# A head's 48 output columns as a 64-row tile of 32 and a shared tile of 16, and x in three PSUM banks

## The chip, the cores and the metric

The kernel runs on one core of a Trainium2 chip. The metric is the time of one execution in microseconds (us), the median of several runs. A smaller number is better. TensorE (PE) does matrix products, VectorE (DVE) and ScalarE (ACT) do elementwise work, GpSimd (POOL) and SyncE (SP) issue DMAs here.

## What is computed

A gated linear attention over 768 steps for 4 batches of 8 heads of width 48, then two feed-forward layers over the 3072 tokens. The inputs are float32.

```python
# attention: q, k, v, alpha are (4, 8, 768, 48)
for t in range(S):
    state = alpha[:, :, t, :, None] * state + np.einsum('bhd,bhe->bhde', k[:, :, t], v[:, :, t])
    y[:, :, t] = np.einsum('bhd,bhde->bhe', q[:, :, t], state)
x = y.transpose(0, 2, 1, 3).reshape(3072, 384)
# layer 1 (384 -> 1536 -> 384)
g = x @ w_gate
x = (g * (1.0 / (1.0 + np.exp(-g))) * (x @ w_val)) @ w_out
# layer 2: x / rms(x) * rms_g first, then the same with its own weights
```

## The kernel before

**Attention.** The work is cut into 24 chunks: 6 blocks of 128 steps for each of 4 batches, with all 8 heads in a chunk. Heads go in 4 pairs (`NP`); a pair's first head lies on partitions 0 to 63 and its second on 64 to 127, of which 48 each are used. Inside a chunk the product over steps is split by levels 1, 2, 4, 8, 16, 32, 64 (`LEVELS`): at level b the second half of each run of 2b steps attends to the first half. The first 6 chunks do all seven levels; the other 18 do the five from 4 up and get the terms of short distance from DVE instead (`CDS`).

For a level, `scores` makes a 64 x 64 score block per head on PE, in tiles of 64 rows by 32 columns; DVE masks it or ACT copies it to SBUF (`masks`, `copies_p`), as P. `outputs` then multiplies v (`vlt`) by P into the PSUM tile `y`, which holds the transposed output x: 384 output columns as partitions of three groups of 128, by 128 steps. A pair has 96 output columns, three blocks of 32 (`blocks32`). The middle block mixes both heads, so v lies in SBUF padded with zeros to 96 columns for either head, and every product uses all 128 rows: 12 matrix products per level, three per pair. `own_terms` writes the terms of the chunk's own steps into `y` by a transpose and adds q times the state (12 more products, with the padded state `Sd`). `kp`, `kt` and `kv` make k transposed and k^T v for the state (`state`), which the chunk of the same batch four later uses. `split_x` copies `y` out as a float32r high part (`xhi`, ACT) and a low part (`xlo`, DVE); that is the input of layer 1.

PSUM before: `y` has one bank, the pool `ps2` has two that scores, `kp`, `kv` and two small tiles of the norm take in turn, and the feed-forward layers have the other five (`g`, `v`, `o0` to `o2`).

**Feed-forward.** Layer 1 goes over 7 blocks of 3 or 4 chunks, layer 2 over 6 blocks of 4. Each block goes over 12 slices of the 1536 hidden columns, and for each slice PE does pieces g, v and o; in layer 1, from the second block on, and in layer 2 each piece is nine products in float32r (high and low parts). The first block uses float32 with six instructions on the chip in a piece. The weights of layer 1 are unpacked by ACT and DVE first (`conv`, lines 150 to 172), and this runs beside the first chunks.

**Order.** All engines run in the order in which the code is written. A chunk is a list of steps T = 0 to 23; `slot` runs the step T of one chunk and T - 12 of the next. Chunks 0 to 2 run alone, and later ones have their slots placed between the pieces of the block before (`run`, `mlp_points`). The steps that matter here: scores of levels 1 to 8 at T = 6 (which is T = 18 of the chunk before), masks at 7, 8 and 10, scores of levels 16 to 64 at 9, `kp` at 12, `kt` at 13, `own_terms` and the first outputs at 14, `kv` and the other outputs at 16, the high part of x and the state at 17, the low part at 18. Waits between engines are put in by the framework from the tiles that instructions share.

Of the kernel before, what the change touches and what calls it, by code (L numbers as in the profile page):

```python
# [55 lines left out]
class Kernel:  # L56


    def __init__(self, tc, ctx, qka, vl, vlx, vn, qn, dirx, w1, w2, g2, mask, ident, zero, out):
# [7 lines left out]
        self.ps2 = self.pool("ps2", 2, space=PSUM)  # L67
# [185 lines left out]

    def scores(self, n, ls):

        nc = self.nc
        qk = self.qk[n % 2]
        sc_all = self.ps2.tile([128, 4, NP, 32], F32, tag="sc", name="sa" if ls[0] < 4 else "sb")
        out = {}
        for i, l in enumerate(ls):  # L260
            b = LEVELS[l]
            if b < CDS[n]:
                continue
            if b < 64:
                sc = out[l] = sc_all[:, i]
                kc = self.kc.pop((n, l))
                qc, kc = kc[:, 0], kc[:, 1]
            else:
                sc = out[l] = sc_all[:, 2:4].rearrange("s g p t -> s (g p t)").rearrange("s (p t) -> s p t", p=NP)
# [33 lines left out]
    def blocks32(self):  # L303

        for cb in range(3 * NP):
            yield cb // 3, slice(32 * (cb % 3), 32 * (cb % 3) + 32), cb // 4, 32 * (cb % 4)

    def own_terms(self, n):

        nc = self.nc  # L310
        Y = self.Y = self.ps.tile([128, KT, C], F32, tag="y", name="y")
        yn = self.yn.pop(n)
        for k in range(KT):
            nc.tensor.matmul(out=Y[:, k], lhsT=yn[:, 128 * k:128 * k + 128], rhs=self.ident, is_transpose=True,  # L314
                             start=(k == 0), stop=False, skip_group_check=True)
        if n >= B:
            for p, e, kt, o in self.blocks32():
                nc.tensor.matmul(out=Y[o:o + 32, kt], lhsT=self.Sd[:, p].rearrange("d h e -> d (h e)")[:, e],  # L318
                                 rhs=self.qk[n % 2][:, 0, p], start=False, stop=False, skip_group_check=True)

    def outputs(self, n, ls):
        for l in ls:
            b = LEVELS[l]
            if b < CDS[n]:
                continue
            pt = self.P.pop((n, l))
            for p, e, kt, o in self.blocks32():
                ov = self.Y[o:o + 32, kt].rearrange("e (j u i) -> e j u i", u=2, i=b)[:, :, 1]
                self.nc.tensor.matmul(out=ov, lhsT=self.vlt[l][:, p, e], rhs=pt[:, p],  # L329
                                      start=False, stop=False, skip_group_check=True)  # L330
        if n == CDS.index(4) - 1:
            self.pxfree = True

    def kv(self, n):

        nc = self.nc
        kv = self.ps2.tile([128, NP, D], F32, tag="sc", name="kv")
        kt, vn = self.kt.pop(n), self.vnt.pop(n)
        for p in range(NP):
            for h in range(2):  # L340
                for o in (64 * h, 64 * h + 32):
                    nc.tensor.matmul(out=kv[o:o + 32, p], lhsT=kt[:, p, o:o + 32], rhs=vn[:, p, h],  # L342
                                     start=True, stop=True, skip_group_check=True)
        self.kvt = kv
# [11 lines left out]
    def split_x(self, m, part):  # L356
        Y = self.Y
# [73 lines left out]
    def chunk(self, n, T):  # L431
# [5 lines left out]
        if T == 12 and more:  # L437

            kp = self.kp = self.ps2.tile([128, NP, 128], F32, tag="sc", name="kp")
            for p in range(NP):  # L440
                nc.tensor.transpose(out=kp[:, p], in_=self.qk[n % 2][:, 1, p], identity=self.ident)  # L441
        if T == 14:
            self.own_terms(n)
            self.outputs(n, range(4))
# [38 lines left out]
        if T == 11 and n >= B:  # L483
            for h in range(2):
                o = slice(64 * h, 64 * h + 64)
                nc.scalar.activation(out=self.Sd[o, :, h], in_=self.Sc[n % B][o], func=AF.Copy)
        if T == 13 and more:
            kt = self.kt[n] = self.a1.tile([128, NP, 128], F32, tag="kt", name="kt")
            nc.scalar.activation(out=kt, in_=self.kp, func=AF.Copy)
# [16 lines left out]
    def norm_steps(self, j):  # L506
# [16 lines left out]
        ss = self.ps2.tile([128, MB], F32, tag="sc", name="ss")  # L523
# [17 lines left out]
        rb = self.ps2.tile([128, NW], F32, tag="sc", name="rb")  # L541
# [125 lines left out]
    def run(self):  # L667
# [16 lines left out]
        self.vlt = [v(0, 96), v(384, 96)] + self.vlt  # L684
# [73 lines left out]
def _layout(inputs):  # L758
    q, k, v, a = (np.asarray(inputs[n]) for n in ("q", "k", "v", "alpha"))
    con = np.ascontiguousarray  # L760
# [11 lines left out]
    for b in LEVELS:  # L772
        x = vt.reshape(NCH, C // (2 * b), 2, b, NP, 2, D)[:, :, 0].reshape(NCH, 64, NP, 2, D)
        o = np.zeros_like(x[:, :, :, 0])
        z = [np.stack([x[:, :, :, 0], o], axis=3), np.stack([o, x[:, :, :, 1]], axis=3)]
        vl.append(np.concatenate(z, axis=1).reshape(NCH, 128, NP, 2 * D))
# [8 lines left out]
    for pre in ("moe_", "moe2_"):  # L785
        wg, wv, wo = (np.asarray(inputs[pre + s]) for s in ("w_gate", "w_val", "w_out"))
        w = [x.reshape(KT, 128, NF, 128).transpose(2, 1, 0, 3).reshape(NF, 128, 384) for x in (wg, wv)]
# [21 lines left out]
```

## Time and profile before

| | |
|---|---|
| median of 3 runs | 1138.23 us (1137.38 to 1142.36) |
| the profiled execution | 1136.99 us |
| its span, first to last instruction | 1135.2 us |
| PE busy | 1084.1 us (95%) |
| DVE busy | 656.4 us (58%) |
| ACT busy | 417.7 us (37%) |
| DMA moved | 112.54 MB |

The profile is of one execution. What lies outside its span is 1.8 us. An engine's busy time counts time in which at least one of its instructions is under way; instructions of PE overlap. A float32 product shows as two instructions in the profile, a float32r one as one.

### The profile page before, as it was taken

The page shows a single profiled execution, that of the slowest core. Times are in us where ns is not written, and L with a number is a line of the kernel's source. Part 1 is how long each engine was busy: PE and PEld are TensorE (multiplying, and loading weights), DVE is VectorE, ACT ScalarE, POOL GpSimd, SP SyncE. Part 2 cuts the span into 40 slices and gives each one's busy share as a digit, 9 for nine tenths or more (in the row PEclk, how much of TensorE's full clock was granted, in tenths as well). Part 3 has the DMA queues.
Part 4 walks back from the last instruction along what each step waited for, and adds up shares of the span by engine and source line. Part 5 has one row for each costly group of instructions (what it writes and reads, how often), then busy time and mean ns, then how long its engine had stood idle before and what let it go on. Part 6 is the DMA issues. An engine that isn't in the chain of part 4 may idle for free.

```text
span 1135.2 us, 29428 instructions
## 1 busy us (share of the span) xinstructions
PE 1084.1 (95%) x12864; PEld 901.0 (79%) x12864; DVE 656.4 (58%) x1361; ACT 417.7 (37%) x749; POOL 46.5 (4%) x81
## 2 busy tenths in 40 slices
PE   2679999999999999999999999999999999999997
PEld 2555569999999988887888888888888888888886
DVE  4789876877678777676746887723322323233221
ACT  3465624543344443343324354432231222322212
POOL 2012000000000000000000000000000000000000
PEclk9689999999999999999999999999999999999999
DMA  9677535443454463444315243110000000100000
GB/s 278 207 213 238 159 99 148 114 125 105 127 166 139 125 173 106 116 127 139 105 58 207 99 152 113 42 56 1 28 28 1 29 28 1 56 1 1 29 1 28
DMA packets 56033, 112.54 MB, mean 99 GB/s; under 512 B 7392, under 2 KB 40672, under 8 KB 55904
## 3 DMA queue, kind: packets, MB, share of 16 engines
q1 hardware_dynamic: 50592, 89.02, 27.1%
q0 software_dynamic: 5312, 21.63, 5.5%
q8 instruction: 101, 1.65, 0.6%
q14 instruction: 28, 0.23, 0.1%
HBM read 97.65 MB, written 12.98 MB: 97 GB/s over the span
## 4 chain that ended last, share of the span: by engine, by line
PE 85%; DVE 2%; DMA 2%; ACT 1%; issue 1%; SPq 0%; DVEq 0%; ACTq 0%; POOLq 0%
PE g L605 25%; PE v L605 25%; PE o L646 25%; PE y L329 3%; PE sb L277 2%; PE y L318 1%; PE sa L277 1%; PE kv L342 1%; PE y L314 1%; PE kp L441 1%; PE rb L544 0%; DMA x2d<-ev 0%; DMA ydd<-yd 0%; PE ss L525 0%; ACT ev L566 0%
## 5 line engine op out<-in xcount | busy, mean ns | idle before, releaser
L615 DVE TENSOR_TENSOR s<-s,v 128x512 f32<-128x512 f32 (+1 forms) x156 | 100.8, 646 | 368.4 <-PE v L605 365.1
L605 PE MATMUL g<-xhi,w 128*128 128x512 f32 (+1 forms) x864 | 282.8, 381 | 0.0
L605 PE MATMUL v<-xhi,w 128*128 128x512 f32 (+1 forms) x864 | 281.8, 380 | 0.0
L646 PE MATMUL o<-hh,w 128*128 128x512 f32 (+1 forms) x864 | 208.7, 377 | 0.0
L621 ACT ACTIVATE hh<-s 128x512 fp32r<-128x512 f32 (+1 forms) x144 | 87.2, 606 | 278.6 <-DVE s L615 278.4
L612 ACT ACTIVATE s<-g 128x512 f32<-128x512 f32 (+1 forms) x156 | 88.1, 565 | 259.3 <-PE g L605 250.6
L605 PEld LDWEIGHTS g<-xhi,w 128*128 128x128 f32 x864 | 161.2, 188 | 27.9
L605 PEld LDWEIGHTS v<-xhi,w 128*128 128x128 f32 x864 | 161.3, 188 | 27.1
L646 PEld LDWEIGHTS o<-hh,w 128*128 128x128 f32 x864 | 160.0, 188 | 25.9
L605 PE MATMUL g<-xlo,w 128*128 128x512 f32 (+1 forms) x432 | 162.6, 376 | 0.0
L605 PE MATMUL v<-xlo,w 128*128 128x512 f32 (+1 forms) x432 | 162.6, 376 | 0.0
L646 PE MATMUL o<-hl,w 128*128 128x512 f32 (+1 forms) x432 | 120.6, 386 | 1.2 <-ACT ev L566 0.8
L627 DVE TENSOR_TENSOR hl<-s,hh 128x512 fp32r<-128x512 f32 (+1 forms) x144 | 94.4, 656 | 42.1 <-ACT hh L621 37.7
L605 PEld LDWEIGHTS g<-xlo,w 128*128 128x128 f32 x432 | 81.2, 188 | 12.8
L605 PEld LDWEIGHTS v<-xlo,w 128*128 128x128 f32 x432 | 81.2, 188 | 12.3
L646 PEld LDWEIGHTS o<-hl,w 128*128 128x128 f32 x432 | 77.7, 188 | 16.6 <-ACT ev L566 2.3
L229 DVE TENSOR_TENSOR qk<-qk,bpb 128x512 f32<-128x512 f32 x96 | 65.7, 685 | 7.0 <-ACT kc L252 4.7
L252 ACT ACTIVATE kc<-qk 128x512 f32<-128x512 f32 x72 | 45.4, 631 | 61.0 <-DVE qk L229 60.3
L329 PE MATMUL y<-pt,vl 128*32 128x64 f32 x2880 | 52.1, 225 | 2.2 <-issue 2.2
L329 PEld LDWEIGHTS y<-pt,vl 128*32 128x32 f32 x2880 | 47.1, 115 | 3.8 <-issue 3.8
L298 ACT ACTIVATE pt<-sb 32x128 f32<-32x128 f32 x96 | 25.7, 268 | 41.1 <-DVE pt L288 40.1
L229 DVE TENSOR_TENSOR qk<-qk,bpa 128x512 f32<-128x512 f32 x48 | 33.0, 687 | 5.0 <-ACT px L252 3.3
(104 smaller groups left out, 1037.7 us busy)
## 6 DMA issues: line engine op xcount, KB each, us to landing
vl<-vl SPq DMA_DIRECT2D x120, 192.0 KB, 4.9
qk<-qka SPq DMA_DIRECT2D x48, 288.0 KB, 5.0
room<-w POOLq DMA_DIRECT2D x36, 384.0 KB, 5.2
dir<-dirx SPq DMA_DIRECT2D x54, 192.0 KB, 3.2
wraw<-w SPq DMA_DIRECT2D x18, 384.0 KB, 3.9
room<-w SPq DMA_DIRECT2D x18, 384.0 KB, 3.9
vn<-vn SPq DMA_DIRECT2D x24, 192.0 KB, 4.2
x2in<-x2d SPq DMA_DIRECT2D x6, 768.0 KB, 4.3
```

The source lines that it names most:

```text
L229: self.nc.vector.tensor_tensor(out=v, in0=v, in1=sub(t, o, [(1, 2), (2, nb), (0, b)]), op=ALU.mult)
L252: self.nc.scalar.activation(out=sub(t, 0, [(NP * 64, 2), (b, NP * 64 // b), (1, b)]), in_=v, func=AF.Copy)
L277: nc.tensor.matmul(out=sc[o:o + 32, p], lhsT=kc[d, p, gs], rhs=qc[d, p, gs if b < 64 else slice(0, 64)], start=True, stop=True, skip_group ...
L298: nc.scalar.activation(out=self.pt32[o:o + 32, :, g], in_=out[NL - 2][o:o + 32], func=AF.Copy)
L314: nc.tensor.matmul(out=Y[:, k], lhsT=yn[:, 128 * k:128 * k + 128], rhs=self.ident, is_transpose=True, start=(k == 0), stop=False, skip_gro ...
L329: self.nc.tensor.matmul(out=ov, lhsT=self.vlt[l][:, p, e], rhs=pt[:, p], start=False, stop=False, skip_group_check=True)
L605: nc.tensor.matmul(out=ps[:, :N], lhsT=a, rhs=x, start=(q == 0), stop=(q == len(ops) - 1))
L612: nc.scalar.activation(out=s[:, :N], in_=g[:, :N], func=AF.Silu)
L615: nc.vector.tensor_tensor(out=s[:, :N], in0=s[:, :N], in1=v[:, :N], op=ALU.mult)
L621: nc.scalar.activation(out=hh[:, :N], in_=s[:, :N], func=AF.Copy)
L627: nc.vector.tensor_tensor(out=hl[:, :N], in0=s[:, :N], in1=hh[:, :N], op=ALU.subtract)
L646: nc.tensor.matmul(out=O[gj][i][:, :N], lhsT=a[:, 128 * i:128 * i + 128], rhs=x[:, :N], start=(f == 0 and q == 0), stop=(f == NF - 1 and q ...
```

## The change

The PSUM tile `Y` is made once, with three banks of 512 columns. Columns 0 to 127 of each bank hold x; what used the pool `ps2` lies in the rest of the same banks: scores (`place_sc`), `kp`, `kv` and, later, the norm's two tiles. The pool `ps2` is gone.

A head's 48 output columns are a block of 32 of its own and one of 16. The block of 32 is a product over that head's 64 rows alone; the two blocks of 16 of a pair share one block of 32 columns and one product over 128 rows. The second head's columns are turned by 16 on the host (`_layout`), in v and in the rows of the first layer's weights, so that the order of output columns in x fits. v needs 64 columns a pair in SBUF in place of 96, and `Sd` 32 in place of 96. The count of products stays 12 per level: four of 128 rows, then eight of 64 rows. Each call of `outputs` does all shared ones of its levels first and then all of 64 rows. The terms of the state come the same way, inside `outputs`.

```diff
-        self.ps2 = self.pool("ps2", 2, space=PSUM)
+        self.Y = self.ps.tile([128, 3, NW], F32, name="Y")
+        self.kvt = self.Y[:, 2, C:C + NP * D].rearrange("d (p e) -> d p e", e=D)
+        self.kp = self.Y[:, 0:2, C:3 * C]
...
-        self.vlt = [ac.tile([128, NP, 2 * D], F32, name=f"vl{i}") for i in range(NL - NX)]
+        self.vlt = [ac.tile([128, NP, 64], F32, name=f"vl{i}") for i in range(NL - NX)]
         self.Sc = [ac.tile([128, NP, D], F32, name=f"S{b}") for b in range(B)]
-        self.Sd = ac.tile([128, NP, 2, D], F32, name="Sd")
+        self.Sd = ac.tile([128, NP, 32], F32, name="Sd")
...
+    def place_sc(self, l):
+        i, c = (l // 2, 1 + l % 2) if l < 4 else (l - 4, 3)
+        return i, slice(c * C, c * C + C)
...
-    def blocks32(self):
-
-        for cb in range(3 * NP):
-            yield cb // 3, slice(32 * (cb % 3), 32 * (cb % 3) + 32), cb // 4, 32 * (cb % 4)
-
     def own_terms(self, n):
 
-        nc = self.nc
-        Y = self.Y = self.ps.tile([128, KT, C], F32, tag="y", name="y")
         yn = self.yn.pop(n)
         for k in range(KT):
-            nc.tensor.matmul(out=Y[:, k], lhsT=yn[:, 128 * k:128 * k + 128], rhs=self.ident, is_transpose=True,
-                             start=(k == 0), stop=False, skip_group_check=True)
-        if n >= B:
-            for p, e, kt, o in self.blocks32():
-                nc.tensor.matmul(out=Y[o:o + 32, kt], lhsT=self.Sd[:, p].rearrange("d h e -> d (h e)")[:, e],
-                                 rhs=self.qk[n % 2][:, 0, p], start=False, stop=False, skip_group_check=True)
-
-    def outputs(self, n, ls):
+            self.nc.tensor.matmul(out=self.Y[:, k, 0:C], lhsT=yn[:, C * k:C * k + C], rhs=self.ident, is_transpose=True,
+                                  start=True, stop=False, skip_group_check=True)
+
+    def outputs(self, n, ls, own=False):
+        mm = lambda o, a, x: self.nc.tensor.matmul(out=o, lhsT=a, rhs=x, start=False, stop=False, skip_group_check=True)
+        ls = [l for l in ls if LEVELS[l] >= CDS[n]]
+        pt = {l: self.P.pop((n, l)) for l in ls}
+        q = self.qk[n % 2][:, 0]
+
+        def y(p, part, l=None):
+            j = 3 * p + part
+            t = self.Y[32 * (j % 4):32 * (j % 4) + 32, j // 4, 0:C]
+            return t if l is None else t.rearrange("e (j u i) -> e j u i", u=2, i=LEVELS[l])[:, :, 1]
+        own = own and n >= B
+        if own:
+            for p in range(NP):
+                mm(y(p, 1), self.Sd[:, p], q[:, p])
         for l in ls:
-            b = LEVELS[l]
-            if b < CDS[n]:
-                continue
-            pt = self.P.pop((n, l))
-            for p, e, kt, o in self.blocks32():
-                ov = self.Y[o:o + 32, kt].rearrange("e (j u i) -> e j u i", u=2, i=b)[:, :, 1]
-                self.nc.tensor.matmul(out=ov, lhsT=self.vlt[l][:, p, e], rhs=pt[:, p],
-                                      start=False, stop=False, skip_group_check=True)
-        if n == CDS.index(4) - 1:
+            for p in range(NP):
+                mm(y(p, 1, l), self.vlt[l][:, p, 32:64], pt[l][:, p])
+        halves = [(p, h, slice(64 * h, 64 * h + 64)) for p in range(NP) for h in range(2)]
+        if own:
+            for p, h, d in halves:
+                mm(y(p, 2 * h), self.Sc[n % B][d, p, 16 * h:16 * h + 32], q[d, p])
+        for l in ls:
+            for p, h, d in halves:
+                mm(y(p, 2 * h, l), self.vlt[l][d, p, 0:32], pt[l][d, p])
+        if n == CDS.index(4) - 1 and NL - 1 in ls:
...
-        kv = self.ps2.tile([128, NP, D], F32, tag="sc", name="kv")
+        kv = self.kvt
...
             self.own_terms(n)
-            self.outputs(n, range(4))
+            self.outputs(n, range(4), own=True)
...
-                nc.scalar.activation(out=self.Sd[o, :, h], in_=self.Sc[n % B][o], func=AF.Copy)
+                nc.scalar.activation(out=self.Sd[o, :, 16 * h:16 * h + 16], in_=self.Sc[n % B][o, :, 32 - 32 * h:D - 32 * h], func=AF.Copy)
```

Below, rows of the program's order (line, operation, output <- inputs, output shape, xcount) show three places; a bracket names the engine or DMA queue whose signal the instruction waits for. In the changed file the lines of the same functions are a few higher.

PE at T = 14 of a chunk with five levels, before: the transposes of the own terms, the state's product, then levels 4 and 8.

```order
L314 MATMUL y<-ident,yn 128x128 [waits DMASW7_49]
L314 MATMUL y<-ident,yn 128x128 x2
L318 MATMUL y<-qk_91,Sd 32x128 x12
L329 MATMUL y<-pt,vl_92 32x16x4 [waits DMAHW1_49]
L329 MATMUL y<-pt,vl_92 32x16x4 x11
L329 MATMUL y<-pt,vl_93 32x8x8 [waits DMAHW2_49]
L329 MATMUL y<-pt,vl_93 32x8x8 x11
```

The same place of another such chunk, with the change: the first rows of four are the shared products, the last three rows those of 64 rows.

```order
L312 MATMUL Y<-ident,yn 128x128 [waits DMASW1_49,Activation_49]
L312 MATMUL Y<-ident,yn 128x128 x2
L316 MATMUL Y<-qk_88,Sd 32x128 x4
L316 MATMUL Y<-pt,vl_90 32x16x4 [waits DMAHW2_49]
L316 MATMUL Y<-pt,vl_90 32x16x4 x3
L316 MATMUL Y<-pt,vl_91 32x8x8 [waits DMAHW3_49]
L316 MATMUL Y<-pt,vl_91 32x8x8 x3
L316 MATMUL Y<-qk_88,S_97 32x128 x8
L316 MATMUL Y<-pt,vl_90 32x16x4 x8
L316 MATMUL Y<-pt,vl_91 32x8x8 x8
```

Twelve products a level have become four and eight, the eight of all levels stand together at the end, and the transposes wait for ACT, whose last use of the tile ahead of them is the copy of k transposed (`kt`, T = 13).

PE at the scores of chunk 5 (T = 6), between pieces g, v and o of the first block, before:

```order
L605 MATMUL v<-x_460,x_122 128x384 [waits DVE_49]
L605 MATMUL v<-x_460,x_122 128x384 x2
L277 MATMUL sa<-px 32x32 [waits PE_49]
L277 MATMUL sa<-px 32x32 x31
L277 MATMUL sa<-kc 32x32 x16
L277 MATMUL sa<-kc 32x32 [waits Activation_49]
L277 MATMUL sa<-kc 32x32 x15
L646 MATMUL o_1244<-s,x_122 128x384
```

The same place with the change:

```order
L612 MATMUL v<-x_453,x_120 128x384 [waits DVE_49]
L612 MATMUL v<-x_453,x_120 128x384 x2
L282 MATMUL Y<-px 32x32 [waits DVE_49]
L282 MATMUL Y<-px 32x32 x31
L282 MATMUL Y<-kc 32x32 x16
L282 MATMUL Y<-kc 32x32 [waits Activation_49]
L282 MATMUL Y<-kc 32x32 x15
L653 MATMUL o_1224<-s,x_120 128x384
```

The scores stand where they stood, and the first of them waits for DVE in place of PE itself. The last DVE instruction ahead of them that uses the tile is the low part of x of chunk 4 (`xlo`).

DVE at the state and the low part of x (T = 17 and 18) of a later chunk, before:

```order
L353 TENSOR_TENSOR S_99<-S_99,bpb 128x192
L354 TENSOR_TENSOR S_99<-S_99,kv 128x192 [waits DVE_49,PE_49]
L229 TENSOR_TENSOR qk_91<-qk_91,bpb 128x2x16x16 [waits Activation_49]
L221 TENSOR_TENSOR bpb<-bpb 128x8
L384 TENSOR_TENSOR dir<-dir 128x96
L384 TENSOR_TENSOR pr<-dir 128x96 [waits DVE_49]
L374 TENSOR_TENSOR xlo<-y,xhi 128x3x128 [waits Activation_49]
```

The same place with the change:

```order
L360 TENSOR_TENSOR S_97<-S_97,bpb 128x192
L361 TENSOR_TENSOR S_97<-S_97,Y 128x192 [waits DVE_49,Activation_49]
L231 TENSOR_TENSOR qk_89<-qk_89,bpb 128x2x16x16
L223 TENSOR_TENSOR bpb<-bpb 128x8
L391 TENSOR_TENSOR dir<-dir 128x96
L391 TENSOR_TENSOR pr<-dir 128x96 [waits DVE_49]
L381 TENSOR_TENSOR xlo<-Y,xhi 128x3x128
```

The addition of k^T v to the state waits for ACT (the high part of x, which ACT copies just ahead from the same tile) where it waited for PE's `kv`; the rest of the order is the same. The scores of level 16 (T = 9) get a wait for DVE's mask of level 8 (T = 8) in the same way.

## Rows read from the trace of the kernel before

**Rows 1.** The page: the chain that ended last, by engine.

```profile
PE 85%; DVE 2%; DMA 2%; ACT 1%; issue 1%; SPq 0%; DVEq 0%; ACTq 0%; POOLq 0%
```

**Rows 2.** Stretches: length, busy (xcount) PE, PEld, DVE, ACT, POOL; clock, DMA, GB/s.

```profile
0.00:70.00 70.00, 32.96 (x1370) 29.29 (x1372) 42.41 (x93) 30.42 (x53) 10.53 (x24) 0.80 0.84 250
155.00:600.00 445.00, 443.29 (x7828) 385.93 (x7817) 314.94 (x777) 173.58 (x370) 23.43 (x36) 1.00 0.46 126
```

**Rows 3.** Timeline of PE, chunk 13: start, us from first to last end.

```profile
352.55 0.86 PE L318 MATMUL y<-qk,Sd 128*32 128x128 f32 x24
353.23 0.85 PE L329 MATMUL y<-pt,vl 128*32 128x64 f32 x48
354.01 0.45 PE L605 MATMUL g<-xhi,w 128*128 128x384 f32 x1
...
355.78 0.55 PE L342 MATMUL kv<-vn,kt 128*32 128x48 f32 x32
356.14 1.19 PE L329 MATMUL y<-pt,vl 128*32 128x64 f32 x72
357.26 0.45 PE L605 MATMUL v<-xhi,w 128*128 128x384 f32 x1
```

**Rows 4.** A stretch of 0.035 us there: busy PE of tile y (instructions under way).

```profile
356.13:356.17 0.04, 0.02 (x4) 1.00 0.00 0
```

**Rows 5.** Timeline of chunks 4 and 5: PE with DVE and ACT.

```profile
121.90 0.49 PE L314 MATMUL y<-ident,yn 128*128 128x128 f32 x3
...
124.69 0.58 ACT L489 ACTIVATE kt<-kp 128x512 f32<-128x512 f32 x1
...
134.07 0.72 PE L277 MATMUL sa<-px 64*32 64x32 f32 x62
...
137.65 0.55 DVE L374 TENSOR_TENSOR xlo<-y,xhi 128x384 fp32r<-128x384 f32 x1
```

**Rows 6.** Timelines at the states of chunks 1, 2 and 3: DVE and ACT.

```profile
51.61 0.69 DVE L229 TENSOR_TENSOR qk<-qk,bpb 128x512 f32<-128x512 f32 x1 [0.34 <-ACT kc L252]
...
52.21 0.49 ACT L368 ACTIVATE x<-y 128x384 f32<-128x384 f32 x1 [0.64 <-PE y L329]
...
68.06 0.48 ACT L368 ACTIVATE x<-y 128x384 f32<-128x384 f32 x1
68.20 0.69 DVE L229 TENSOR_TENSOR qk<-qk,bpb 128x512 f32<-128x512 f32 x1 [0.64 <-ACT kc L252]
...
99.30 0.35 DVE L350 COPY S<-kv 128x192 f32<-128x192 f32 x1
...
100.19 0.48 ACT L372 ACTIVATE xhi<-y 128x384 fp32r<-128x384 f32 x1
```

**Rows 7.** Timelines of chunks 1 and 2: DVE's masks of levels 8 and 16.

```profile
42.54 0.42 DVE L288 TENSOR_TENSOR pt<-sb,mask 128x256 f32<-128x256 f32 x1 [2.71 <-PE sb L277]
...
57.09 0.42 DVE L288 TENSOR_TENSOR pt<-sa,mask 128x256 f32<-128x256 f32 x1
...
58.48 0.42 DVE L288 TENSOR_TENSOR pt<-sb,mask 128x256 f32<-128x256 f32 x1
```

**Rows 8.** Stretch of chunk 2's scores of levels 16 to 64: busy PE.

```profile
55.32:57.28 1.96, 1.94 (x96) 0.50 0.27 46
```

**Rows 9.** Timeline of chunk 14 and the scores of chunk 15.

```profile
376.99 0.35 DVE L354 TENSOR_TENSOR S<-S,kv 128x192 f32<-128x192 f32 x1
377.86 0.49 ACT L372 ACTIVATE xhi<-y 128x384 fp32r<-128x384 f32 x1 [0.56 <-PE y L329]
379.69 0.55 DVE L615 TENSOR_TENSOR s<-s,v 128x384 f32<-128x384 f32 x1 [1.21 <-PE v L605]
380.16 0.55 DVE L374 TENSOR_TENSOR xlo<-y,xhi 128x384 fp32r<-128x384 f32 x1
...
381.08 1.07 PE L277 MATMUL sa<-kc 64*32 64x32 f32 x64
```

More of the change, by code (lines that the diff above doesn't have):

```diff
@@ L264, in scores @@
             if b < 64:
-                sc = out[l] = sc_all[:, i]
+                sc = out[l] = self.Y[:, *self.place_sc(l)].rearrange("s (p t) -> s p t", p=NP)
                 kc = self.kc.pop((n, l))
@@ L268, in scores @@
             else:
-                sc = out[l] = sc_all[:, 2:4].rearrange("s g p t -> s (g p t)").rearrange("s (p t) -> s p t", p=NP)
+                sc = out[l] = self.Y[:, 2, C:3 * C].rearrange("s (p t) -> s p t", p=NP)
                 qc, kc = qk[:, 0, :, 64:128], qk[:, 1, :, 0:64]
@@ new lines, in outputs @@
+    def outputs(self, n, ls, own=False):
[11 more added lines that the diff above has]
+                mm(y(p, 1), self.Sd[:, p], q[:, p])
+        for l in ls:
+            for p in range(NP):
[4 more added lines that the diff above has]
+                mm(y(p, 2 * h), self.Sc[n % B][d, p, 16 * h:16 * h + 32], q[d, p])
+        for l in ls:
+            for p, h, d in halves:
+                mm(y(p, 2 * h, l), self.vlt[l][d, p, 0:32], pt[l][d, p])
+        if n == CDS.index(4) - 1 and NL - 1 in ls:
@@ L342, in kv @@
                     nc.tensor.matmul(out=kv[o:o + 32, p], lhsT=kt[:, p, o:o + 32], rhs=vn[:, p, h],
-                                     start=True, stop=True, skip_group_check=True)
-        self.kvt = kv
+                                     start=False, stop=True, skip_group_check=True)
     def state(self, n):
@@ L437, in chunk @@
         if T == 12 and more:
-            kp = self.kp = self.ps2.tile([128, NP, 128], F32, tag="sc", name="kp")
             for p in range(NP):
-                nc.tensor.transpose(out=kp[:, p], in_=self.qk[n % 2][:, 1, p], identity=self.ident)
+                nc.tensor.transpose(out=self.kp[:, p // 2, C * (p % 2):C * (p % 2) + C], in_=self.qk[n % 2][:, 1, p],
+                                    identity=self.ident)
         if T == 14:
             self.own_terms(n)
-            self.outputs(n, range(4))
+            self.outputs(n, range(4), own=True)
         if T == 16:
@@ L522, in norm_steps @@
         yield
-        ss = self.ps2.tile([128, MB], F32, tag="sc", name="ss")
+        ss = self.Y[:, 0, 0:MB]
         for c in range(MB):
@@ L540, in norm_steps @@
         yield
-        rb = self.ps2.tile([128, NW], F32, tag="sc", name="rb")
+        rb = self.Y[:, 1]
         for c in range(MB):
@@ L759, in _layout @@
     q, k, v, a = (np.asarray(inputs[n]) for n in ("q", "k", "v", "alpha"))
+    turn = np.roll(np.arange(D), 16)
+    v = np.stack([v[:, 0::2], v[:, 1::2][..., turn]], axis=2).reshape(v.shape)
+    head = np.arange(DM).reshape(NP, 2, D)
+    order = np.stack([head[:, 0], head[:, 1][:, turn]], axis=1).ravel()
     con = np.ascontiguousarray
@@ L786, in _layout @@
         wg, wv, wo = (np.asarray(inputs[pre + s]) for s in ("w_gate", "w_val", "w_out"))
+        if pre == "moe_":
+            wg, wv = wg[order], wv[order]
         w = [x.reshape(KT, 128, NF, 128).transpose(2, 1, 0, 3).reshape(NF, 128, 384) for x in (wg, wv)]
```

14 lines of the change are left out of this document (6 added, 8 removed).

## The prediction

> **What bounds the kernel now.** I read the page's chain first, then stretches, then single chunks. The chain that ended last is PE for 85% [rows 1], so PE comes first. But the stretches are of two kinds [rows 2]. From 155 to 600 us PE is busy 443.29 of 445 us at full clock: what PE does less of there comes off the end, one for one. In the first 70 us PE is busy for 32.96 us only, at a mean clock of 0.80, and DVE has the most work (42.41 us). Up to about 145 us PE runs ahead of the others: chunk 5's scores (T = 6) start at 134.07, before `xlo` of chunk 4 has been made, which ends at 137.65 + 0.55 = 138.20 [rows 5]. Less PE work gains nothing there, and a longer wait between DVE and ACT can cost in full. So the change is to be summed in two ledgers: PE's time in the later chunks, and waits in the early ones.
>
> **What the products cost.** Chunk 13 shows it [rows 3]. Two levels (48 instructions) start at 353.23 and the next piece at 354.01: 0.78 us. Three levels (72) take 357.26 - 356.14 = 1.12 us. So a level costs 0.34 us and each call 0.78 - 0.68 = 0.10 us besides, which I read as the price of going over from 128 x 32 tiles to 128 x 128. A level's 24 instructions are 12 products of two. Four of them start within 0.035 us [rows 4], which is what four column tiles side by side look like; so a level is 6 sets of four, of 0.34 / 6 = 0.056 us each. The state's product takes 353.23 - 352.55 = 0.68 us, 6 sets of 0.113.
>
> After the change a level has 4 shared products (2 sets of four) and 8 of 64 rows. By the index arithmetic in the diff, these 8 fall on all eight places of four columns by two row halves, and the two of one column write to different banks. If they go side by side, they are 2 sets of eight, each still 0.056 us. A level is then 4 sets in place of 6: 0.112 us less. The state's product saves 2 x 0.113 = 0.226 us.
>
> What is added on PE is one change of tile shape, 128 x 32 to 64 x 32, in each call of `outputs`, two a chunk. No row has this change. Its bounds: nothing, since from `kv` (another size of output, same tiles) to `y` there is no gap beyond the pace (32 instructions in 0.36 us, [rows 3]); and 0.21 us, if it costs 0.10 us like the change to 128 x 128 and the way back as much again. I take 0.10, as the nearest row that changes the shape: 0.20 us a chunk.
>
> A chunk with five levels: 5 x 0.112 + 0.226 - 0.20 = 0.58 us less. There are 18 (chunks 6 to 23): 10.5 us. Chunk 5 has seven levels, 0.81 us. **Gain 11.3 us.** With a free switch it is 15.1 us (19 x 0.20 more), with the upper bound 7.1 us (38 x 0.11 less).
>
> **What the shared banks cost.** The tile `Y` now carries x, scores, `kp` and `kv`, and the order shows new waits of one user for another's.
>
> PE's lead. The transposes of chunk 4 start at 121.90 and must now wait for ACT's `kt`, which ends at 124.69 + 0.58 = 125.27: 3.4 us. The scores of chunk 5 start at 134.07 and must wait for `xlo` of chunk 4, until 138.20: 4.1 us [rows 5]. Behind either wait PE holds the pieces g, v and o of the first block. The two are not added, since both only bring PE back to where DVE and ACT are; the larger one counts. **Loss 4.1 us.**
>
> The early stage, where DVE and ACT pass work to each other. The state now waits for ACT's copy of x out of the same tile [rows 6]. In chunk 1 the state (0.35 us, as in chunk 3) could start at 51.26, just ahead of the row at 51.61, and now starts after 52.21 + 0.49 = 52.70; it ends at 53.05 in place of 51.61: 1.44 us. In chunk 2, 68.06 + 0.48 + 0.35 - 68.20 = 0.69 us. In chunk 3, 100.19 + 0.48 - 99.30 = 1.37 us. And the scores of level 16 and up now wait for the mask of level 8. In chunk 2 that mask ends at 57.09 + 0.42 = 57.51 [rows 7]; the scores take 1.94 us, at a granted clock of 0.50, that is 1.2 GHz [rows 8]; so the next mask starts at 59.45 in place of 58.48: 0.97 us. Chunk 0 has the same waits, but chunk 1's mask stands 2.71 us for its scores [rows 7], which takes them up. Sum 1.44 + 0.69 + 1.37 + 0.97 = **4.5 us**, if nothing is made good later. Bounds: 0, as one of the engines may have room before 145 us; and 6.1 us, if chunk 0's (1.6, an estimate from the same durations) come on top.
>
> The later chunks. The same state wait exists in all of them, and I cost it at nothing for this cover [rows 9]: in chunk 14 the state stood at 376.99 and must go behind `xhi`, 377.86 + 0.49 = 378.35, so DVE is 1.36 us later. Behind it DVE has an idle 1.21 us before s, and the scores of chunk 15 start 0.37 us after `xlo` ends (381.08 against 380.71): 1.58 us of room. It is thin: of 1.36 us, 0.15 us eats into those 0.37. Were the cover gone, the scores would be late and with them all of PE.
>
> Fewer bytes of v (a DMA that no row of the chain waits for; DMA is 2% there, [rows 1]) and shorter copies into `Sd` (ACT, busy 173.58 of 445 us, [rows 2]) change nothing on the path.
>
> **Sum:** 4.1 + 4.5 - 11.3 = -2.7 us. The profiled execution took 1136.99 us, 1.24 below the median of the runs; the difference is taken over to both: 1134.3, and 1138.23 - 2.7 = **1135.5 us**. Its own range, from the bounds of the switch (-3.8 to +4.2) and of the early stage (-4.5 to +1.6), each about half used: 1130 to 1140.
>
> **Rivals.**
>
> *The two row halves of a column take turns* (slower). Then the 8 products are 4 sets of four, a level is 6 sets as before, and the shape changes come on top: 19 x 0.20 + 8.6 = +12.4 us: 1150.6. For it: no row of this trace has two row tiles in one column; the scores, which use 64 x 32 tiles, put the halves in different columns by line 277's slices. Against it: four tiles start within 0.035 us [rows 4], so the instruction queue alone does not forbid eight in 0.07. The forecast's gain over no change, 2.7 us, is spread over 97 levels (18 x 5 + 7), 0.028 us each, and a level has two sets of eight: from 0.056 + 0.014 = 0.070 us a set on, the change stops gaining. Chance 0.17.
> The Trainium skill ("TensorE: Matmul & The Clock Gate", section "Wait — 56ns, not 53.3ns?") says that matmuls start no closer than about 25 ns however small they are. By that rule 24 instructions would take 0.60 us before and after and nothing would be saved, as in this rival. The trace disagrees where columns are side by side: four starts in 0.035 us, 24 in 0.34 [rows 3, 4].
> The same page's section "Measured speedup vs the span model" gives some 4 ns for each further tile packed beside others; by that, eight tiles fit into a set of 0.056 us as forecast. No run so far shows eight.
>
> *Eight at once, but not in one set's time.* The nearest row for a pace of starts is `kv`: 32 in 0.36 us, 0.0113 each [rows 3]. 16 instructions would then take 0.18 in place of 0.112 us, and a level saves 0.044. With the state's saving whole: 18 x (0.22 + 0.226 - 0.20) + 0.33 = 4.8 us gain, net +3.8: 1142.0. Chance 0.14.
>
> *The early waits do not reach the end* (faster). ACT and DVE make up their 4.5 us while PE waits elsewhere: -11.3 + 4.1 = -7.2: 1131.0; with a free switch 1127.2. For it: DVE is busy only 42.41 of the first 70 us [rows 2]; against it, the rows of masks and merges follow one another with waits for ACT in between [rows 6]. Chance 0.24.
>
> *The thin cover fails.* If the state's wait holds up PE in each of 18 later chunks by 1 of its 1.36 us: +18 - 2.7, 1153. For it: room of 1.58 against 1.36 us only [rows 9]. Chance 0.05.
>
> **Chances and range.** The forecast has 0.40. A change below 0.5% (5.7 us) can hardly be told from none here. Faster by more than that: the third rival, and the lowest part of the forecast's own range, 0.31. Slower by more: the first rival, the last and a part of the second, 0.26. The rest, 0.43. From 1127 (third rival, free switch) to 1149 the range leaves out the greater part of the first rival and all of the last, and a little below, some 0.2.
>
> **What the new profile would show.** In the late chunks: y of 72 instructions in about 1.12 - 0.34 + 0.10 = 0.88 us, with a set of eight starting within some 0.056 us; a gap of about 0.10 us between its 128 x 32 and 64 x 32 rows; no wait of `sa` for `xlo`. In chunk 4 PE waits at the transposes for ACT, in chunk 5 at the scores for DVE. The stretch in which PE is always busy starts some 8.6 us later, and from there to the end is 11.3 us shorter. I am wrong if y of three levels takes 1.2 us or more, if the busy stretch starts at the same time, or if PE waits in late chunks for DVE.

## The result, and the profile after

The changed kernel takes 1146.94 us (1145.71 to 1148.09, 4 runs), the kernel before 1138.32 in the same rounds: a ratio of 1.0069, with an interval of 1.0042 to 1.0095. It is slower, by 8.6 us. The profiled execution took 1148.09 us, 11.1 above the profiled one of before, so the trace has some 2.5 us more to explain than the medians.

Where they part is read from one event that every chunk has, the start of the own terms' transposes on PE (T = 14). With the change it stands later than before by 1.90, 4.42, 7.66 and 10.10 us in chunks 0 to 3, by 13.47 in chunk 4 and 14.02 in chunk 5. From there on it comes back slowly: 13.22 in chunk 19, 11.47 in chunk 23, 11.06 at the last instruction. So 10.1 us are lost up to chunk 3, 3.9 in chunks 4 and 5, and 3.0 come back after that. The idle time of PE behind chunk 5 is the same in both traces (2.0 us, 1.9 before), so no wait makes up the 3.0; they are the products'.

The two stretches of [rows 2] again, the second moved by 14 us, in the same columns:

```profile
0.00:70.00 70.00, 27.73 (x1125) 22.03 (x1125) 38.74 (x84) 26.19 (x47) 10.56 (x24) 0.79 0.71 205
169.00:614.00 445.00, 443.23 (x7832) 382.43 (x7816) 313.98 (x777) 173.38 (x373) 23.44 (x36) 1.00 0.43 115
```

In the first 70 us PE, DVE and ACT have done less than before: 1125 PE instructions in place of 1370, 84 on DVE in place of 93. They wait more. In the later stretch PE is as busy as before and gets through almost the same number of instructions (7832, 7828 before): the same work takes nearly the same time. In between, from 70 to 85 us, the mean granted clock is 0.71 with the change (a part at 1.2 GHz, the rest at 2.4) and 1.00 before; PE was busy for less of the time ahead of it.

PE in chunk 13, which answers to [rows 3]:

```profile
366.18 0.42 PE L316 MATMUL Y<-qk,Sd 128*32 128x128 f32 x8
366.42 0.41 PE L316 MATMUL Y<-pt,vl 128*32 128x64 f32 x16
366.75 0.45 PE L316 MATMUL Y<-qk,S 64*32 64x128 f32 x16
367.00 0.61 PE L316 MATMUL Y<-pt,vl 64*32 64x64 f32 x32
367.54 0.44 PE L612 MATMUL g<-xhi,w 128*128 128x384 f32 x1
...
369.32 0.55 PE L350 MATMUL Y<-vn,kt 128*32 128x48 f32 x32
369.69 1.17 PE L316 MATMUL Y<-pt,vl 128*32 128x64 f32 x72
370.79 0.44 PE L612 MATMUL v<-xhi,w 128*128 128x384 f32 x1
```

Eight tiles do go side by side: the state's 16 instructions of 64 rows take 367.00 - 366.75 = 0.25 us, and its 8 of 128 rows, in fours, take 0.24. But the 32 that follow take 0.54 to the next piece, about 0.40 without the change of shape, where four sets of eight at 0.056 would be 0.22. The first call takes 367.54 - 366.18 = 1.36 us (1.46 before), the second 1.10 (1.12 before): 0.12 us less a chunk, where 0.58 was forecast.

PE and what it waits for in chunk 0, from the timeline (the bracket is the idle time ahead of the row and what ended it), with ACT and DVE where they are the ones waited for:

```profile
26.22 0.38 ACT L306 ACTIVATE pt<-Y 128x256 f32<-128x256 f32 x1
...
26.66 1.11 PE L447 MATMUL Y<-ident,qk 128*128 128x128 f32 x4 [2.18 <-ACT pt L306]
...
27.81 0.60 ACT L496 ACTIVATE kt<-Y 128x512 f32<-128x512 f32 x1 [0.64 <-PE Y L447]
...
28.46 0.90 PE L312 MATMUL Y<-ident,yn 128*128 128x128 f32 x3 [0.69 <-ACT kt L496]
...
35.04 0.47 ACT L375 ACTIVATE x<-Y 128x384 f32<-128x384 f32 x1
35.55 0.36 DVE L357 COPY S<-Y 128x192 f32<-128x192 f32 x1 [0.99 <-ACT x L375]
...
35.96 0.72 PE L282 MATMUL Y<-px 64*32 64x32 f32 x62 [2.15 <-DVE S L357]
```

In the trace of before the same three stand at 25.68 (`kp`), 26.55 (transposes) and 31.92 (scores of chunk 1, of which a part comes only at 34.90, after 2.38 us of idle time). `kp` now waits for the last copy of P, since both are in one tile; the transposes wait for `kt`; x is copied only then; the state waits for x; and the next chunk's scores wait for the state. What ran in three places runs in one row, and DVE's next masks come 1 us later for it, and the masks of level 16 2.1 us. The waits of PE in the first 100 us, summed (us in total, times, longest):

```profile
PE Y L282 <- DVE pt L293: 11.1, 3, 5.8
PE Y L447 <- ACT pt L306: 6.5, 3, 2.2
...
PE Y L282 <- DVE S L357: 4.1, 3, 2.1
PE Y L312 <- ACT kt L496: 4.1, 4, 1.2
```

None of the four is among the waits of before. But PE stood ahead of scores and `kp` then too, for 26.6 and 8.2 us in the first 90 us; now it is 34.5 and 6.5, and the 4.1 ahead of the transposes are new. And in chunk 4 its scores meet the low part of x of chunk 3:

```profile
112.94 0.55 DVE L381 TENSOR_TENSOR xlo<-Y,xhi 128x384 fp32r<-128x384 f32 x1
...
113.55 1.08 PE L282 MATMUL Y<-px 64*32 64x32 f32 x64 [5.29 <-DVE xlo L381]
```

That wait alone is not the 3.4 us that chunk 4 loses (13.47 - 10.10). Between the transposes of chunks 3 and 4 PE stood before as well, ahead of pieces g and v:

```profile
PE v L605 <- DVE s L615: 3.5, 4, 1.8
PE g L605 <- ACT s L612: 0.7, 1, 0.7
```

These 4.2 us are gone with the change, which has 5.29 here and 0.35 ahead of chunk 4's transposes: 1.4 us more. The rest is the granted clock. With PE standing these 5.29 us it falls to 0.50, that is 1.2 GHz, where it was 1.00 before (the change, then the same pieces before, in the columns of [rows 2]):

```profile
112.84:119.65 6.81, 6.10 (x135) 4.22 (x136) 6.52 (x12) 3.10 (x3) 1.90 (x3) 0.50 0.52 175
100.73:107.54 6.81, 6.40 (x26) 3.17 (x18) 6.78 (x12) 5.88 (x7) 1.91 (x3) 1.00 0.51 170
```

The piece o behind the scores takes 4.00 us to the next piece with the change:

```profile
115.41 4.21 PE L653 MATMUL o<-s,x 128*128 128x384 f32 x6
119.41 2.23 PE L612 MATMUL g<-x,x 128*128 128x384 f32 x6
```

Before, it takes 2.07, 1.9 us less:

```profile
100.73 2.20 PE L646 MATMUL o<-s,x 128*128 128x384 f32 x6
102.80 2.20 PE L605 MATMUL g<-x,x 128*128 128x384 f32 x6
```

### The profile page after: what moved, and what is told of

The parts are those of the page before. It is cut to its first block, busy times and chain, and to the rows that moved or that the text cites. A ratio compares the mean times of both kernels' runs of the same rounds, so it can differ in the third digit from the quotient of the medians.

```text
span 1146.3 us, 29415 instructions
## 1 busy us (share of the span) xinstructions
PE 1083.5 (95%) x12864; PEld 894.1 (78%) x12864; DVE 654.6 (57%) x1361; ACT 415.1 (36%) x749; POOL 46.6 (4%) x81
## 4 chain that ended last, share of the span: by engine, by line
PE 86%; DVE 3%; DMA 1%; ACT 1%; issue 1%; SPq 0%; DVEq 0%; ACTq 0%; POOLq 0%
PE o L653 25%; PE g L612 25%; PE v L612 25%; PE Y L316 4%; PE Y L282 3%; PE Y L350 1%; DVE x L168 1%; PE Y L312 1%; PE Y L447 1%; DMA yn<-ydd 1%; PE Y L551 0%; DVE qk L231 0%; DMA ydd<-yd 0%; PE Y L532 0%; ACT x L152 0%
## 5 line engine op out<-in xcount | busy, mean ns | idle before, releaser
L634 DVE TENSOR_TENSOR hl<-s,hh 128x512 fp32r<-128x512 f32 (+1 forms) x144 | 94.3, 655 | 40.9 <-ACT hh L628 37.5
L316 PE MATMUL Y<-pt,vl 64*32 64x64 f32 (+1 forms) x2880 | 55.5, 230 | 2.3 <-issue 2.3
L316 PEld LDWEIGHTS Y<-pt,vl 64*32 64x32 f32 (+1 forms) x2880 | 46.1, 112 | 6.4 <-issue 4.1
L282 PEld LDWEIGHTS Y<-kc 64*32 64x32 f32 x2304 | 25.8, 113 | 28.6 <-issue 14.4
L282 PE MATMUL Y<-kc 64*32 64x32 f32 x2304 | 31.4, 201 | 15.3 <-DVE pt L293 11.1
```

The lines of the kernel that those rows point to most:

```text
L316: mm = lambda o, a, x: self.nc.tensor.matmul(out=o, lhsT=a, rhs=x, start=False, stop=False, skip_group_check=True)
L634: nc.vector.tensor_tensor(out=hl[:, :N], in0=s[:, :N], in1=hh[:, :N], op=ALU.subtract)
```

## The experiments

The theory from the two traces: the layout loses 14 us by waits up to chunk 5, and the products gain 0.12 us a chunk, because beyond 32 instructions of 64 rows in a row the pace of eight is not kept. The rivals: the 64-row products themselves cost the early time; or the end of a call is slow in any case.

**The layout without the products.** The kernel before, with `Y` in three banks, scores, `kp` and `kv` placed as in the change, and the old 12 products a level.

```diff
-        self.ps2 = self.pool("ps2", 2, space=PSUM)
+        self.Y = self.ps.tile([128, 3, NW], F32, name="Y")
-                ov = self.Y[o:o + 32, kt].rearrange(...)
+                ov = self.Y[o:o + 32, kt, 0:C].rearrange(...)
```

> The layout of the change (x in three PSUM banks that also hold scores, kp and kv) with the products of the kernel before: 12 of 128 rows a level, v padded to 96 columns. Theory (the shared banks make the loss, by their waits in chunks 0 to 4; the new products give back only 0.12 us a chunk): the transposes of chunk 5 start at about 167 us as with the change (152.9 before), and the time is that of the change plus its small gain, 1146.9 + 18 x 0.12 = 1149. Rival (the 64-row products cost the time in the early chunks, by their order or at the low clock): 1138 to 1140, transposes of chunk 5 at about 153.

1150.26 us, ratio 1.0111 (1.0096 to 1.0126). Transposes 10.65 us late in chunk 3 and 14.75 in chunk 5. The whole early loss is there without one 64-row product; the theory's 1149 is met, and the products are worth 3.3 us to the changed kernel. Nor is the early loss the granted clock's: up to chunk 3's transposes it is at 0.50 for 27.3 us before, 37.5 with the change and 30.7 here, and these 3.4 us more at half speed can cost PE no more than 1.7 of the 10.65.

**At most 32 in a row.**

```diff
-            self.outputs(n, range(4), own=True)
+            self.outputs(n, range(3), own=True)
+        if T == 15:
+            self.outputs(n, range(3, 5))
...
-            self.outputs(n, range(4, NL))
+            self.outputs(n, range(5, NL))
```

> The change, with the outputs of a chunk in three calls in place of two (state and level 4; levels 8 and 16; levels 32 and 64), so that a call has at most 32 instructions of 64 rows in the chunks with five levels. Theory (the first 32 instructions of 64 rows in a call keep the pace of eight in 0.056 us, and what comes after them starts at a half to a third of it): no call has a slow rest, a chunk's calls take 0.89 + 0.67 + 0.67 = 2.22 us in place of 2.46, 18 x 0.24 = 4.3 us less: 1142.6. Rival (the last level of any call is slow, however many stand ahead of it): each call keeps its slow end and there is one more change of tile shape: 0.2 to 0.3 us a chunk more, 1151 to 1152.

1147.01 us, ratio 1.0081 (1.0066 to 1.0096): as fast as the change, which neither the theory nor the rival had. The calls of chunk 13 in its timeline, the first two (one right behind the other) and the last, two levels:

```profile
365.23 0.42 PE L316 MATMUL Y<-qk,Sd 128*32 128x128 f32 x8
...
366.93 0.45 PE L614 MATMUL g<-xhi,w 128*128 128x384 f32 x1
...
369.09 0.79 PE L316 MATMUL Y<-pt,vl 128*32 128x64 f32 x48
369.81 0.45 PE L614 MATMUL v<-xhi,w 128*128 128x384 f32 x1
```

0.72 us for two levels; before, two took 0.78 [rows 3]. In the change a third level in the same call makes 1.10 of it: 0.38 us for that level, more than the 0.34 of before. So the slow rest is gone where a call has 32 instructions of 64 rows, and it is not the end of a call that is slow. But 0.72 is 0.27 us more than 8 sets of 0.056, for the two changes of shape in the call (128 x 32 to 64 x 32, and on to 128 x 128); before, 0.78 was 0.11 more than 12 sets, for one. A third call brings two more changes, and they take back most of what the slow rests of the two calls had cost, 0.34 us (1.36 and 1.10 less the sets and 0.27 each): 1.70 + 0.72 = 2.42 us in place of 2.46, so 0.04 us remain in this chunk. In chunks 6 to 8 a piece of the layer stands between the first two calls, and from chunk to chunk the transposes come no earlier at all, where with the change they come 0.12 us earlier.

**Early chunks out of the shared banks.** Scores, `kp` and `kv` of chunks 0 to 2, and the first scores of chunk 3, go to the banks of `o2`, `g`, `v` and `o0`, which are free until the first block.

```diff
+        if ls[0] < 4 and n <= 3:
+            early = self.ps.tile([128, NW], F32, tag="o2", name="sa")
+        elif ls[0] >= 4 and n <= 2:
+            early = self.ps.tile([128, NW], F32, tag="g", name="sb")
...
+            self.kp = (self.ps.tile([128, NW], F32, tag="v", name="kp")... if n <= 2 else self.Y[:, 0:2, C:3 * C])
```

> The change, but in chunks 0 to 2 (which run ahead of the first feed-forward block) scores, kp and kv lie in the five banks that the feed-forward layers use later, and the first scores of chunk 3 too; from chunk 3 on as in the change. Theory (the waits come from sharing banks with x): what chunks 0 to 2 lose goes (the transposes of chunk 3 start 10.1 us later than before with the change, 96.44 against 86.34), and chunks 3 and 4 still lose some 3.9: 1146.9 - 10.1 = 1136.8. Rival (the early loss is from the products, or what is won at chunk 3 is lost again at chunk 4, where PE has to wait in any case): 1144 to 1147.

1140.89 us, ratio 1.0022 (1.0011 to 1.0032). Transposes of chunk 3 at 87.01, 0.67 us later than before in place of 10.10: the loss of the early stage is the shared banks. The time falls by 6.0 us, not by 10.1; the profiled runs lie 7.0 apart. At chunk 5 this kernel is still 9.4 us ahead of the change, but later waits take some of that: behind chunk 5 it gains 0.5 us on the kernel before, where the change gains 3.0, and from 170 to 600 us PE waits 3.9 us in it (1.9 for `ev`, 1.3 for the load of `yn`, 0.7 "issue") and 1.6 with the change. After chunk 3 the loss of chunk 4 comes as it did, with the same wait and a granted clock of 0.50 from 102.5 to 109.3 us:

```profile
104.14 1.08 PE L289 MATMUL Y<-px 64*32 64x32 f32 x64 [5.29 <-DVE xlo L389]
```

**Both.** The last two edits together.

> Both edits together: the early chunks' scores, kp and kv in the feed-forward banks, and the outputs in three calls. If both theories hold, the savings lie in different stretches and add: 1146.9 - 10.1 - 4.3 = 1132.5, below both kernels. If only the first holds, 1137 to 1142.

1141.44 us, ratio 1.0030 (1.0018 to 1.0041): the third call adds nothing, as it added nothing alone.

**`kp` alone.** Of those edits only the one of `kp`: chunks 0 to 2 have it in the bank of `v`.

> The change, with kp alone of chunks 0 to 2 in a feed-forward bank; scores and k^T v stay in the banks of x. Theory (waits that the prediction left out, kp behind the copies of P and the transposes behind kt, make up about half of the early loss): the transposes of chunk 3 start about 5 us earlier than with the change, at 91 to 92, and the time is 1146.9 - 4 to 5 = 1142 to 1143. Rival (the waits that were priced, the state behind x and the scores behind masks, are the loss, and each chunk catches up with whatever is earlier): under 1 us gained, 1146 to 1147.

1143.05 us, ratio 1.0038 (1.0023 to 1.0053). Transposes of chunk 3 at 90.86, 4.53 us late in place of 10.10. So 5.6 of the 10.1 us are `kp`'s bank, which the prediction had not priced, and 3.9 (from 4.53 to 0.67) are those of scores and `kv`, which it had priced at 4.5. (Scores and `kv` alone were not moved, so the split holds in this order.) In this trace `kp` no longer waits for the copies of P, and of the waits for `kt` 1.2 us are left of 4.1. What is left are the scores' waits for the masks (11.6 us in three) and for the state (8.3 in three); the longest of the latter:

```profile
36.45 0.79 PE L282 MATMUL Y<-px 64*32 64x32 f32 x41 [4.31 <-DVE S L357]
```

**One call for all levels, first form.** Three runs: the change, the change with the early banks, and the kernel before.

```diff
         if T == 16:
+            self.own_terms(n)
             if more:
                 self.kv(n)
-            self.outputs(n, range(4, NL))
+            self.outputs(n, range(NL), own=True)
-            for l in {15: (0, 1, 2), 16: (3,), 17: (4,), 18: (5,), 19: (6,)}.get(T, ()):
+            for l in {16: (0, 1, 2), 17: (3, 4), 18: (5,), 19: (6,)}.get(T, ()):
```

> The change, with all the outputs of a chunk in one call at T = 16 (own terms, k^T v, then all shared products, then all of 64 rows), and the loads of v for the next chunk one step later. Theory (a call pays two changes of tile shape, and beyond 32 instructions of 64 rows a set of eight takes about 0.08 us, which is still less than two sets of four at 0.056): read from chunk 5's seven-level call, a five-level chunk takes 1.88 + 0.11 + 0.15 = 2.14 us in place of 1.37 + 1.10 = 2.47, 18 x 0.33 = 5.9 us less; and the transposes no longer meet kt of the same chunk, which takes away chunk 4's wait of 3.4 us: 1146.9 - 9.3 = 1137.6. Rival (the slow rest gets slower the longer the run of 64-row instructions): no gain per chunk, 1143.5 from chunk 4's wait alone.

> One call at T = 16 together with the feed-forward banks for scores, kp and kv of chunks 0 to 2. Theory: the early loss is gone (that run was at 1140.9), chunk 4's 3.4 and 18 x 0.33 = 5.9 us come off: 1131.6, clearly below the kernel before. Rival (no gain per chunk): 1137.5.

> The kernel before, products and banks unchanged, with the outputs of a chunk in one call at T = 16 as in the two runs beside it. It tells what the single call is worth without 64-row products. Theory: one change of tile shape less a chunk, 18 x 0.10 = 1.8 us: 1136.8. If the place of the call itself matters (fewer interruptions of the feed-forward pieces, or later x), it shows here too, as more or less than that.

1150.87, 1144.39 and 1153.32 us. They don't answer the question: the load of q and k for the chunk after next stands at T = 15, ahead of the call, so the state's product read q of that later chunk and PE waited for its load (in the second run, from 100 to 600 us):

```profile
PE Y L323 <- DMA qk<-qka: 5.7, 4, 2.8
```

**One call, second form.** The same with that load behind the call.

```diff
-        if T == 15 and n + 2 < NCH:
+        if T == 16 and n + 2 < NCH:
             self.load_qk(n + 2)
```

> One call at T = 16 and the feed-forward banks for chunks 0 to 2 as in the run before it, with the load of q and k of the chunk after next one step later too, so that the state's product reads its own q and PE doesn't wait for a load. Theory (a five-level chunk takes 2.14 us for its products in place of 2.47 with the change, chunk 4's wait for kt of 3.4 us is gone, the early waits are gone): from the 1140.9 us of the run with the banks alone, 3.4 + 5.9 less: 1131.6. Rival (a single long call delays x and the next scores, or the later load arrives late, and PE waits there instead): 1137 or more.

> The kernel before with one call at T = 16, and the same later load of q and k. Theory: one change of tile shape less a chunk, 18 x 0.10 = 1.8 us: 1136.7. If it is faster than that by 2 us or more, what the single call brings is not from the 64-row products; if it is slower than before, the single call itself costs.

With the early banks and the new products 1137.68 us, ratio 1.0001 (0.9992 to 1.0010); with the kernel before 1144.39, ratio 1.0056 (1.0045 to 1.0068). The call of a later chunk in the first of the two:

```profile
378.16 0.40 PE L323 MATMUL Y<-qk,Sd 128*32 128x128 f32 x8
378.38 0.74 PE L323 MATMUL Y<-pt,vl 128*32 128x64 f32 x40
379.05 0.45 PE L323 MATMUL Y<-qk,S 64*32 64x128 f32 x16
379.30 1.09 PE L323 MATMUL Y<-pt,vl 64*32 64x64 f32 x80
380.32 0.45 PE L622 MATMUL v<-xhi,w 128*128 128x384 f32 x1
```

2.16 us, as expected (2.14), in place of 2.46. The 80 instructions of five levels take about 0.9 us without the change of shape, 0.09 a set of eight: slower than 0.056, still faster than two sets of four. The single call itself costs, though: with the old products it made the kernel 5.9 us slower, and in both runs PE has new waits in which the profile shows nothing that it waits for ("issue"; here the first of the two, from 90 to 600 us):

```profile
PE Y L323 <- issue: 6.8, 6, 1.6
PE v L622 <- DVE s L632: 3.4, 2, 2.3
```

In these 510 us the waits called "issue" are 8.0 us with the new products, 10.2 with the old ones, and none in the kernel before. The trace shows what ends them. Queue q8, kind "instruction", makes 101 transfers of 16 KB, one in some 7 us here, and the eight waits of the run with the new products each end 2.3 to 2.6 us after one of them starts (with the old ones, eight of nine end 2.3 to 3.0 us after). For one of them the transfer starts between 421.50 and 421.60 us (first row: packets, MB, share of that time), and PE stops in the middle of the 80:

```profile
q8 instruction: 1, 0.02, 60.2%
...
422.07 0.85 PE L323 MATMUL Y<-pt,vl 64*32 64x64 f32 x55
423.88 0.43 PE L323 MATMUL Y<-pt,vl 64*32 64x64 f32 x25 [0.96 <-issue]
```

So PE stood until a piece of code had come; six of the eight times it did so in the one long call. That is read from the times, and no run tested it.

Between two kernels with one call each the kernel with 64-row products is 6.7 us faster, in spite of the shared banks from chunk 3 on. The rows give 0.29 us a chunk for it (2.16 us in place of 2.45), 5.2 for 18 chunks, and the waits for code are 2.2 us less. The single call takes it back: it cost 5.9 us with the old products.

**The loss in chunk 4.** First the own terms and the first call one step later, behind `kt` (T = 15; the loads behind them move along), then, in the other run, the scores of levels 1 to 8 one step later, behind `xlo` of the chunk before (T = 7, their masks at T = 8); both with the early banks.

> The feed-forward banks for chunks 0 to 2, and the first of the two calls at T = 15 in place of 14, so that the transposes stand a step behind kt. Theory (chunk 4's 3.4 us are the transposes' wait for kt, with the pieces of the first block queued behind): 1140.9 - 3.4 = 1137.5. Rival (PE only comes back to where DVE and ACT are, and waits the same time one step later, at chunk 5's scores): 1140 to 1141.

> The feed-forward banks for chunks 0 to 2, and in all chunks the scores of levels 1 to 8 one step later (T = 7, one step behind the low part of x of the chunk before), their masks all at T = 8. Theory (chunk 4's loss is PE standing 5.29 us at these scores for the low part of x of chunk 3, with pieces of the first block behind them): a step is about one piece of 2 us, which PE now does first: 1140.9 - 2 = 1139, and the wait shrinks from 5.3 to about 3. Rival (DVE and ACT set the pace there, so that PE waits as long at the next place): 1140 to 1142.

1140.99 us, ratio 1.0027 (1.0018 to 1.0036), and 1142.68, ratio 1.0043 (1.0031 to 1.0055). Neither brings the 3.4 us back. In the first the wait for `kt` is gone, and PE stands at the scores of chunks 4 and 5 for 4.30 and 1.51 us (5.29 and 0.93 without the edit). In the second the wait at the scores is shorter, the one at chunk 4's transposes grows from 0.78 to 3.08, and the time is 1.8 us more:

```profile
106.69 0.80 PE L289 MATMUL Y<-px 64*32 64x32 f32 x63 [3.37 <-DVE xlo L389]
...
128.10 0.90 PE L319 MATMUL Y<-ident,yn 128*128 128x128 f32 x3 [3.08 <-ACT kt L504]
```

It is the rival of both: moving one meeting point moves the wait to the next. And neither gets rid of the slow clock. It is 0.50 behind the scores in both (103.5 to 110.3 us, and 107.2 to 110.6), and in the second once more behind the 3.08 us at the transposes (127.7 to 131.1).

**The step for the scores, with one call.**

> The same step for the scores, with one call at T = 16 and the later load of q and k. If the theory holds here too, 1137.7 - 1.5 to 2 = 1136, below the kernel before (1138.5); by the rival 1137.7 again.

1137.27 us, ratio 0.9995 (0.9986 to 1.0004): level with the kernel before, not below it. No version here beats it.

## Why the prediction was wrong

It forecast 2.7 us less; the profiled execution took 11.1 more. Two of its three terms failed, and the third has the right size by luck. By the start of the transposes:

| term | forecast | measured |
|---|---|---|
| gain of the products | 11.3 | 3.0 |
| early stage | 4.5 | 10.1 |
| PE's lead in chunks 4 and 5 | 4.1 | 3.9 |

*The gain.* The step "2 sets of eight, each still 0.056 us" failed, though not the way its rivals had it. Eight tiles do start in the time of four (0.25 us for the state's 16), so the rival of turns is out. But the pace holds for the first 32 instructions of 64 rows in a row only (read one by one, the 33rd or 34th comes late in every call of the later chunks, the state's 16 counted in); a steady chunk has 48 in each call, and the third level costs 0.38 us in place of 0.22. The rival of a slower pace came nearest: its 0.18 us for 16 instructions is what the long call shows (0.09 a set of eight). It took the price from `kv` and spread it over all, so it had 4.8 us of gain against 3.0. The price of a change of shape was too low: a call pays 0.27 us for two changes where it paid 0.11 for one, 0.16 more and not 0.10, and a two-level call with nothing else in it gains 0.06 us where these prices gave 0.12. Together that is what a chunk lacks: of 0.46 us between 0.58 and 0.12, the slow rests are 0.34 and the changes of shape 0.12.

The Trainium skill ("TensorE: Matmul & The Clock Gate", section "Measured speedup vs the span model") gives some 4 ns for each further tile packed beside others. The state's 16 instructions agree with it in so far as eight tiles take little more time than four (0.25 against 0.24 us), with starts 6 to 7 ns apart; the third level of a call does not.

The prediction took the pace of four starts in 0.035 us [rows 4] as one that lasts. The trace of before could have given a warning, but not the price. The scores are 64 x 32 tiles too, and 64 instructions of them take 0.69 us to the next piece in 17 of the 18 later chunks, as here:

```profile
216.10 0.76 PE L277 MATMUL sa<-kc 64*32 64x32 f32 x64
216.78 0.44 PE L646 MATMUL o<-hl,w 128*128 128x384 f32 x1
```

That is some 9 ns each without a change of shape. By it 16 instructions would take 0.147 us in place of 0.112, and the gain would have been about 8 us (an estimate): less than 11.3, still far from 3.0. The row in [rows 9], at 381.08, is the exception: 1.00 us, with 0.32 us in it between two starts.

*The early stage.* The step that failed is the list of waits. Two kinds were priced, the state behind x and the scores behind a mask, at 4.5 us; the runs put these at 3.9 (scores and `kv` out of the banks, on top of `kp`). `kp` behind the copies of P was not in the list, and the transposes behind `kt` were priced for chunk 4 alone, where they count in the early chunks: 5.6 us by the run that frees `kp`. The list was made for DVE's waits, one by one. But `kp`, own terms, x, state and next scores are one chain through one tile, and a wait on PE at its head passes to ACT, DVE and back to PE.

*PE's lead.* The size, 3.9 for 4.1, is luck. The step that failed is the place and the kind of loss. The prediction had PE stand 3.4 us at chunk 4's transposes or 4.1 at chunk 5's scores; there it stands 0.35 and 0.92. The meeting that decides is chunk 4's scores with `xlo` of chunk 3, which was not priced. And PE had little lead to lose in chunk 4: it stood 4.2 us before as well, so its idle time there grows by 1.4 us only. The other 1.9 of chunk 4's 3.4 us are work at a granted clock of 0.50 behind the 5.29 us of idle time, a term that the sum did not have. Chunk 5 adds 0.55.

*The later chunks.* The cover held. The state waits for ACT in all of them, and PE waits in 169 to 614 us no more than it did (443.23 us busy of 445). The rival of the thin cover is out.

*The rival of a free early stage* is out as well: the waits reached the end. Of the 10.1 us at chunk 3, the run with early banks got back 9.4 there, and 6.0 at the end, where later waits had taken the rest.

*The signs of being wrong.* None of the three came: y of three levels took 1.10 us and not 1.2, the busy stretch did start later, and PE doesn't wait for DVE in late chunks. A gain of 3.0 us in place of 11.3 set off none of them.

## What to carry to other kernels

When buffers that rotated are put into one tile, write down every user of the tile in the order of a whole turn and follow the chain around once; waits priced one by one leave out those between two engines that seemed to have room. A pace read from a burst of a few instructions is a bound, not a price: look in the same trace for the longest run of the same tile shape, in more than one chunk. A new wait costs what it adds to the idle time that was there before, and what comes behind it: here 5.29 us of standing added 1.4 us, and 1.9 more at a lower granted clock. And when many short instructions are put into one run, look in the new trace for waits called "issue" and for the transfers of code ahead of them.

## What the runs showed of the hardware

Eight 64 x 32 tiles that write to different PSUM banks run side by side at full clock: 16 instructions of 128 columns take 0.25 us, where 8 on 128 x 32 tiles take 0.24. In runs of 64-row instructions with 64 columns the first 32 go at the pace of eight in 0.056 us; the two sets that follow in a call of 48 take about 0.14 us each, and ten sets in a row 0.09 on average; why it is 32 was not settled. Going from 128 x 32 tiles to 64 x 32 and on to 128 x 128 costs a call 0.27 us, from 128 x 32 straight to 128 x 128 0.11. Behind 5.29 us in which PE stood, its granted clock was 0.50 (112.84 to 119.65 us), and a piece of six instructions took 4.00 us in place of 2.07. Where all outputs of a chunk stood in one call (144 instructions and more), PE stopped for up to 1.6 us at a time, and started again 2.3 to 2.6 us after the start of a 16 KB transfer of the queue that the profile calls "instruction".
